# Pooled attention and a feed-forward in Strassen form: the first pass's sums, the Mish tiles and the written orders

## The chip, the cores and the metric

The program runs on one core of a Trainium2 chip. Counted is the device time in microseconds, median of three runs. The engines are TensorE (PE), VectorE (DVE), ScalarE (ACT), GpSimd (POOL) and SyncE (SP, which here only issues DMAs). Each works its own queue in order; semaphores tie the queues together.

## What is computed

```python
q_pool = q.reshape(B, H, S // 2, 2, D).mean(axis=3)          # B, H, S, D = 4, 8, 1152, 64
attn = softmax(q_pool @ k.T / sqrt(D))                       # per head, 576 x 1152
x = (attn @ v).transpose(0, 2, 1, 3).reshape(2304, 512)
h = x @ w_in                                                 # 512 -> 2048
out = (h * tanh(softplus(h))) @ w_out                        # Mish, 2048 -> 512
```

q, k, v and the output are float32, the two weights float64.

## The kernel before

**Attention.** 32 steps (four batches, four pairs of heads, two halves of the queries). A step i has nine chunks of keys. `QK(i, c)` forms scores in one of two PSUM tiles, `CP` (ACT) copies them to SBUF, `MX`/`MXF` (DVE) keep a running maximum, `MT`, `TMAX`, `MB` turn it into one maximum per query, `SUB` (DVE) and `EXP` (ACT) form the weights, `PV` (PE) multiplies by v, `ADD` (POOL, and for n = 2 a DMA that adds) sums the weights, `FIN0` (PE) adds them over the partitions, and `FLN`, `FEX`, `FC`, `FE`, `FT`, `FU`, `FX` divide and write the result into the large SBUF tile xT (512 x 2304, transposed). For the last two steps `LX` (DVE: an addition, a reciprocal, a product) does the division instead.

**Feed-forward, first pass (the border).** The tokens are cut in six tiles u of 256 for a start; with them the first two of sixteen column blocks f of w_in are done directly: `split_h`/`split_l` cut x into a high and a low part, `H_(u, f)` makes 12 matmuls of 128x256 into an h tile of PSUM (four buffers), `A_g` and `A_gh` (ACT) apply Mish twice (once in full into the SBUF tile g, once rounded into gh), `D_gl` (DVE) forms the rest gl = g - gh, and `O_(u, f)` makes 6 matmuls of 128x512 with w_out. `EVP(u, t)` (ACT) copies the partial sum of 128 tokens out of PSUM into a tile ev, and SP writes it to a DRAM tile part[n], n = 2u + t. The PSUM pairs of O_ take turns, so O_(u, 0) needs the copies of tile u - 2.

**Feed-forward, second phase.** Three groups tp of 768 tokens and eight pairs fp of column blocks make 22 units (tp, fp); the pairs fp = 0 of tp = 0 and 1 are the first pass. A unit is one 2x2 Strassen-Winograd product for the first layer. `XS(tp, n)` (DVE) forms the four differences T1 to T4 of x, each 128x768, from xT (T2 needs T1, T4 needs T2), in three buffers tf; `XH`/`XL` split them. `HP(u, i)` makes seven products of 6 matmuls of 128x384 in PSUM tiles ma, mb, mc; `CPY` and `CC` combine them; `GH` (rounded, to SBUF) and `GG` (in full, in place in PSUM) apply Mish and `GL` forms the rest. `OT(u, n)` makes 6 matmuls of 128x512 for each of six blocks of 128 tokens, with the columns of Gh and Gl as weights and woh, wol as the moving operand. `EV(u, n)` adds the block into xT, which now is the accumulator. Before the first unit of a group adds, `LDP(tp)` (SP) loads the group's six partial sums from part into xT. In group 0 the weights of each unit come as float64 halves in pieces of 512 KB (ri, ro; two buffers); `conv(n, m)` turns a piece into float32 (ACT for m = 0, 1, DVE for m = 2, 3), and conv(n, 3) also issues, on SP, the load of piece n + 2 and a write of the result to DRAM. `SS`, `WH`, `WL` form the unit's weights in the Strassen sums, high and low.

**Order.** The order is written out: each step has a due time in the lists FILL, STEP, END (attention), EDGE (the border, the first and last units of the groups) and STEADY (the units between, with a fixed distance of 15.42), the lists are sorted together, and each engine gets its steps in that order. Pools of SBUF grow from the left and from the right; `reuse_lead` closes the first pass's pools (x3, x2, ag, w0) and opens g, sixteen tiles of 1,536 bytes for Gh and Gl, directly below the pool xp.

The lines that the rows name: 163 QK, 173 CP, 184 MX, 188 MXF, 237 ADD, 267 FIN0, 294 the reciprocal in LX, 389 and 392 the loads of ro and ri, 429 to 454 conv, 992 H_, 996 A_g, 1000 A_gh, 1004 D_gl, 1022 O_, 1027 and 1028 EVP, 1057 XS, 1078 LDP, 1120 HP, 1134 GG, 1138 GH, 1141 GL, 1156 OT, 1165 and 1167 EV.

Of the kernel before, what the change touches and what calls it, by code (L numbers as in the profile page):

```python
# [8 lines left out]
F32 = mybir.dt.float32  # L9
# [9 lines left out]
def f32(ap):  # L19
    return ap.bitcast(F32)  # L20
# [3 lines left out]
def tile_pooled_attention_then_winograd_ffn(ctx: ExitStack, tc: tile.TileContext, q, k, v, moe_w_in, moe_w_out, out):  # L24
# [47 lines left out]
    if True:  # L72
# [1230 lines left out]
        EDGE = [  # L1303
            (-13.0330, FIN0, 28),
            (-12.6895, EXP, 30, 0),
            (-12.3201, PV, 29, 7),
            (-12.0293, FU, 27),
            (-11.8317, FT, 27),
            (-11.1537, EXP, 30, 1),
            (-10.9073, PVE, 29),  # L1310
            (-10.7457, MX, 31, 3),
            (-10.6938, MX, 31, 4),
            (-10.6866, QK, 31, 5),
            (-10.6568, FLN, 28),
            (-10.3955, SUB, 30, 2),
            (-10.0428, QK, 31, 6),
            (-9.8865, CP, 31, 5),
            (-9.8744, FX, 27),
            (-9.0670, ADD, 30, 0),
            (-8.9770, PV, 30, 0),  # L1320
            (-8.8741, FC, 28),
            (-8.5939, MX, 31, 5),
            (-8.4872, MX, 31, 6),
            (-8.4709, CP, 31, 6),
            (-8.3566, QK, 31, 8),
            (-8.2718, ADD, 29, 3),
            (-8.2711, FEX, 28),
            (-8.2122, QK, 31, 7),
            (-8.0969, SUB, 30, 3),
            (-7.8370, EXP, 30, 2),  # L1330
            (-7.8368, ADD, 29, 4),
            (-7.6090, CP, 31, 8),
            (-7.3915, MX, 31, 8),
            (-7.2454, MX, 31, 7),
            (-7.2076, reuse_qk),
            (-7.0445, PV, 30, 4),
            (-6.5484, PV, 30, 2),
            (-6.4867, split_h, 3, 2),
            (-6.0919, split_l, 3, 2),
            (-5.7490, PV, 30, 5),  # L1340
            (-5.7338, split_h, 3, 0),
            (-5.4196, CP, 31, 7),
            (-5.2127, PV, 30, 1),
            (-5.1721, ADD, 30, 1),
            (-5.1571, MXF, 31),
            (-4.6980, FE, 28),
            (-4.6428, split_h, 4, 0),
            (-4.5310, split_h, 3, 3),
            (-4.4512, FU, 28),
            (-3.9977, MT, 31),  # L1350
            (-3.5935, EXP, 30, 3),
            (-3.5625, ADD, 30, 2),
            (-3.3583, split_h, 4, 1),
            (-3.1474, FIN0, 29),
            (-3.1319, TMAX, 31),
            (-2.9496, split_h, 4, 2),
            (-2.5840, FLN, 29),
            (-2.4205, PV, 30, 3),
            (-2.4066, FEX, 29),
            (-2.1443, split_h, 3, 1),  # L1360
            (-1.9834, MB, 31),
            (-1.8885, SUB, 31, 0),
            (-1.8191, split_h, 4, 3),
            (-1.6307, PV, 30, 6),
            (-1.5130, EXP, 31, 0),
            (-1.2737, SUB, 31, 1),
            (-1.0879, SUB, 31, 2),
            (-0.4317, PV, 30, 7),
            (-0.0860, PV, 30, 8),
            (0.4023, PVE, 30),  # L1370
            (0.5731, EXP, 31, 1),
            (1.0951, H_, 1, 0),
            (1.2725, H_, 0, 1),
            (1.2827, PV, 31, 2),
            (1.9519, split_l, 3, 0),
            (2.1706, split_l, 4, 1),
            (2.2210, H_, 0, 0),
            (2.2881, split_l, 3, 1),
            (2.7888, SUB, 31, 3),
            (2.9710, split_l, 4, 3),  # L1380
# [60 lines left out]
            (16.8182, split_h, 5, 2),
            (16.8931, conv, 5, 1),
            (17.1764, conv, 4, 2),
            (17.2002, split_h, 5, 0),
            (17.3767, conv, 4, 3),
            (17.4440, split_h, 5, 3),
            (17.9332, conv, 5, 2),
            (17.9528, A_gh, 2, 0),
            (18.0820, split_l, 5, 1),
            (18.5279, conv, 5, 3),  # L1450
            (18.5785, O_, 1, 1),
            (18.6459, EVP, 1, 0),
            (18.8540, D_gl, 2, 0),
            (19.2055, H_, 3, 0),
            (19.4107, split_l, 5, 3),
            (19.8397, split_l, 5, 0),
            (20.3631, A_gh, 3, 1),
            (20.7401, split_l, 4, 2),
            (20.7904, A_g, 3, 0),
            (20.8692, H_, 4, 0),  # L1460
            (21.1001, O_, 2, 0),
            (21.5031, split_l, 5, 2),
            (22.0276, XS, 0, "T1"),
            (23.2741, D_gl, 2, 1),
            (23.6050, A_gh, 3, 0),
            (23.7571, XS, 0, "T2"),
            (23.7621, EVP, 0, 0),
            (23.8913, H_, 5, 1),
            (24.2332, XH, 0, "T1"),
            (24.2446, conv, 6, 0),  # L1470
            (24.6680, A_g, 4, 0),
# [660 lines left out]
```

## Time and profile before

| | us |
|---|---|
| median of 3 runs | 815.37 |
| lowest and highest | 813.34, 815.38 |
| the profiled execution | 812.05 |
| its span, first to last instruction | 810.3 |
| PE busy | 785.6 |
| DVE busy | 627.0 |
| ACT busy | 605.7 |
| POOL busy | 598.6 |

The rows further down come from the profiled execution. Attention ends near 422 us, the border runs to about 444, the units follow to 805. "Idle before" is the time for which the engine stood before an instruction, and behind the arrow stands what released it. PEclk is the granted share of TensorE's full clock (2.4 GHz). Matmuls overlap, so the time of one is read from the distance of two starts.

### The profile page before, as it was taken

To read this page: it belongs to the slowest core of one execution; us is meant where nothing else is said; L and a number is where in the kernel's file an instruction comes from. 1 tells how busy PE (TensorE), PEld (TensorE's weight loads), DVE (VectorE), ACT (ScalarE), POOL (GpSimd) and SP (SyncE) were. 2 spreads that over 40 slices of the span, in tenths; PEclk is the share of its full clock that TensorE was granted. 3 is DMA by queue.
4 is the path that set the end of the run, shared out by engine and by line. 5 is a ranking of instruction groups with operands and counts; after the bars stand their busy time and mean duration, and the time that the engine had idled before them with its cause. 6 is when DMAs were issued, how large, how long until landed. Compare 5 with 4: busy or idle time off the path is not lost.

```text
span 810.3 us, 13588 instructions
## 1 busy us (share of the span) xinstructions
PE 785.6 (97%) x4991; PEld 547.9 (68%) x4991; DVE 627.0 (77%) x809; ACT 605.7 (75%) x1026; POOL 598.6 (74%) x461
## 2 busy tenths in 40 slices
PE   7899999999999999999899799999999999999997
PEld 4455455555555554554478698898899888888985
DVE  5999999999999999999778579876564574245444
ACT  6999999999999999999857777776544564644441
POOL 4779998898898898898892756668765697666550
PEclk9999999999999999999999999999999999999999
DMA  7567557546656556555246866652722113311302
GB/s 261 161 164 192 134 133 176 121 135 151 156 144 170 118 139 147 137 141 105 59 88 215 294 206 195 213 165 79 194 78 80 53 52 129 106 53 52 104 27 78
DMA packets 47441, 109.40 MB, mean 135 GB/s; under 512 B 3984, under 2 KB 19600, under 8 KB 47376
## 3 DMA queue, kind: packets, MB, share of 16 engines
q1 hardware_dynamic: 37584, 58.99, 22.5%
q0 software_dynamic: 4608, 28.31, 17.8%
q10 hardware_dynamic: 5184, 21.24, 7.8%
q8 instruction: 39, 0.64, 0.3%
q14 instruction: 26, 0.21, 0.1%
HBM read 63.96 MB, written 16.25 MB: 99 GB/s over the span
## 4 chain that ended last, share of the span: by engine, by line
PE 82%; DMA 5%; DVE 5%; POOL 3%; ACT 2%; issue 2%; SPq 0%; ACTq 0%; DVEq 0%; POOLq 0%
PE O L1156 22%; PE s L163 19%; PE pv L245 16%; PE ma L1120 11%; PE mc L1120 6%; PE mb L1120 3%; PE Sb L267 2%; DMA acc<-TB 2%; PE mt L199 2%; DMA ri<-in_moe_w_in_dram 1%; DVE rmax L184 1%; DMA part<-ev 1%; PE Mb L216 1%; POOL acc L237 1%; DVE TA L222 1%
## 5 line engine op out<-in xcount | busy, mean ns | idle before, releaser
L163 PE MATMUL s<-qT,kT 64*128 64x288 f32 x1152 | 204.2, 451 | 4.8 <-ACT TA L173 2.5
L163 PEld LDWEIGHTS s<-qT,kT 64*128 64x128 f32 x1152 | 92.5, 187 | 101.3 <-DVE rmax L184 27.2
L173 ACT COPY TA<-s 128x576 f32<-128x576 f32 x192 | 117.8, 638 | 22.4 <-PE s L163 16.0
L222 DVE TENSOR_TENSOR TA<-TA,Mb 128x1152 f32<-128x1152 f32 x96 | 128.9, 1347 | 1.7 <-PE Mb L216 0.8
L1167 DVE TENSOR_TENSOR xT<-xT,O 128x512 f32<-128x512 f32 x126 | 83.4, 683 | 50.3 <-PE O L1156 49.1
L245 PE MATMUL pv<-TA,vn 128*64 128x288 f32 x768 | 115.7, 422 | 1.4 <-ACT TA L226 1.3
L226 ACT ACTIVATE TA<-TA 128x1152 f32<-128x1152 f32 x96 | 112.8, 1176 | 2.4 <-DVE TA L222 1.8
L231 POOL TENSOR_TENSOR acc<-TA 128x1152 f32<-128x1152 f32 x32 | 85.0, 2657 | 35.5 <-PE s L163 19.0
L1156 PE MATMUL O<-woh,Gh 128*128 128x512 f32 x264 | 104.5, 396 | 2.4 <-DVE xT L1167 2.3
L1156 PE MATMUL O<-woh,Gl 128*128 128x512 f32 x264 | 104.4, 395 | 0.0
L1156 PE MATMUL O<-wol,Gh 128*128 128x512 f32 x264 | 104.3, 395 | 0.0
L1088 POOL TENSOR_TENSOR wS<-wS 128x256 f32<-128x256 f32 x84 | 64.9, 780 | 46.6 <-DMA wS<-spill 38.7
L184 DVE TENSOR_TENSOR rmax<-s,rmax 128x576 f32<-128x576 f32 x128 | 93.2, 749 | 2.1 <-ACT TB L173 0.9
L237 POOL TENSOR_TENSOR acc<-acc 128x576 f32<-128x576 f32 x64 | 91.8, 1434 | 3.9 <-DMA acc<-TB 2.6
L1101 POOL TENSOR_TENSOR wol<-wO,woh 128x1024 fp32r<-128x1024 f32 x22 | 54.3, 2468 | 38.1 <-ACT woh L1097 38.1
L245 PEld LDWEIGHTS pv<-TA,vn 128*64 128x64 f32 x768 | 47.1, 137 | 49.0 <-issue 9.1
L1101 POOL TENSOR_TENSOR wbl<-wS,wbh 128x1024 fp32r<-128x1024 f32 x22 | 53.0, 2407 | 28.3 <-ACT wbh L1097 28.3
L1124 ACT COPY s<-ma 128x384 f32<-128x384 f32 x44 | 21.1, 481 | 66.3 <-PE ma L1120 66.3
L222 DVE TENSOR_TENSOR TB<-TB,Mb 128x1728 f32<-128x1728 f32 x32 | 62.2, 1944 | 0.0
L173 ACT COPY TB<-s 128x576 f32<-128x576 f32 x96 | 59.7, 654 | 2.3 <-DVE rmax L184 2.1
L245 PE MATMUL pv<-TB,vn 128*64 128x288 f32 x384 | 61.1, 414 | 0.0
L1156 PEld LDWEIGHTS O<-woh,Gh 128*128 128x128 f32 x264 | 49.5, 187 | 13.3 <-DVE xT L1167 3.7
(236 smaller groups left out, 1766.9 us busy)
## 6 DMA issues: line engine op xcount, KB each, us to landing
acc<-TB POOLq DMA_DIRECT2D x32, 864.0 KB, 6.3
ri<-in_moe_w_in_dram SPq DMA_DIRECT2D x16, 512.0 KB, 4.0
ro<-in_moe_w_out_dram SPq DMA_DIRECT2D x16, 512.0 KB, 4.1
wS<-spill SPq DMA_DIRECT2D x30, 256.0 KB, 2.9
wO<-spill SPq DMA_DIRECT2D x30, 256.0 KB, 4.1
qn<-in_q_dram ACTq DMA_DIRECT2D x12, 576.0 KB, 5.6
kT<-in_k_dram ACTq DMA_DIRECT2D x12, 576.0 KB, 3.9
vn<-in_v_dram ACTq DMA_DIRECT2D x12, 576.0 KB, 4.2
```

The lines of the kernel that those rows point to most:

```text
L163: pe.matmul(s[:, j, 0:HQ], kT[64 * j:64 * j + 64, c], qT[64 * j:64 * j + 64, hf], start=True, stop=True,)
L173: act.copy(T(i, c), ss[i, c])
L184: dve.tensor_tensor(ss[i, c] if c == FOLD else r, ss[i, c], x, ALU.max)
L222: dve.tensor_tensor(x, x, Mbs[i].unsqueeze(1).to_broadcast([P, w, W]), ALU.subtract)
L226: act.activation(x, x, AF.Exp, scale=0.0625)
L231: pool.tensor_tensor(accs[i][:, 0:2], T(i, 0, 2), T(i, 2, 4), ALU.add)
L237: pool.tensor_tensor(accs[i][:, 0], accs[i][:, 0], accs[i][:, n - 2], ALU.add)
L245: pe.matmul(pvs[i][64 * j:64 * j + 64, 0:HQ], vn[:, j, c, :], T(i, c)[:, j], start=(pvn[i] == 1), stop=(pvn[i] == NC),)
L1101: (dve if e == "dve" else pool).tensor_tensor(l, w_part(u, q), f32(h), ALU.subtract)
L1120: pe.matmul(o, a, b, start=(new and m == 0), stop=(last and m == len(seq) - 1), skip_group_check=True)
L1156: pe.matmul(o, x, y[:, f], start=(f == 0 and m == 0), stop=(f == 1 and m == 2))
L1167: dve.tensor_tensor(acc, acc, o, ALU.add)
```

## The change

`EVP` for n < 6, the tokens of group 0, copies its partial sum straight into xT; nothing is written to part and `LDP(0)` is gone (`LDP(1)` stays). All four T differences have a buffer of their own. The copies overwrite what XS reads, so XS T1, T2, T4 now stand before the first EVP and T3 before the others. `A_g` works in place in the h tile, after `A_gh`, and `D_gl` reads g from PSUM; the SBUF tiles g (four of 1,024 bytes) are gone. A pool pad of 64 bytes is opened between xp and g, so that all Gh and Gl tiles lie 64 bytes lower. EDGE and both lists of STEADY get new times, which changes the order on all engines from step 31 of the attention on; the steps are the same but for LDP(0).

```diff
-        def A_g(u, f):
-            ch[u, f] = pools["ag"].tile([P, UT], F32, tag="g", name=f"g{u}_{f}")
-            act.activation(ch[u, f], hs[u, f], AF.Mish)
-
         def A_gh(u, f):
             gs[u, f] = [pools["ag"].tile([P, UT], F32R, tag="gh", name=f"gh{u}_{f}")]
             act.activation(gs[u, f][0], hs[u, f], AF.Mish)
 
+        def A_g(u, f):
+            act.activation(hs[u, f], hs[u, f], AF.Mish)
+
         def D_gl(u, f):
             gl = pools["ag"].tile([P, UT], F32R, tag="gl", name=f"gl{u}_{f}")
-            dve.tensor_tensor(gl, ch.pop((u, f)), f32(gs[u, f][0]), ALU.subtract)
+            dve.tensor_tensor(gl, hs[u, f], f32(gs[u, f][0]), ALU.subtract)
             gs[u, f].append(gl)
...
         def EVP(u, t):
             n = u * (UT // P) + t
+            if n < KT:
+                act.copy(xT[:, :, n * P:(n + 1) * P], os_[u][t].rearrange("p (a b) -> p a b", b=P))
+                return
             e = pools["ev"].tile([P, DM], F32, tag="ev", name=f"ev{n}")
...
-            t = pools["xt"].tile([P, 2, TH], F32, tag="tf", bufs=3, name=f"{n}f{tp}")
+            t = pools["xt"].tile([P, 2, TH], F32, tag="tf", bufs=4, name=f"{n}f{tp}")
...
         def reuse_lead():
             close("x3", "x2", "ag", "w0")
+            open_pool("pad", 1, side="right").tile([P, 16], F32, name="pad")
             open_pool("g", 8, side="right")
...
-            (42.2186, LDP, 0),
...
```

Of the orders, what the prediction speaks of, by engine. PE from step 31's last chunk on: before H_(1,0), H_(0,1), ..., FIN0(31), O_(0,0), O_(0,1), O_(1,0), O_(1,1), ...; after H_(0,1), H_(1,1), ..., H_(0,0), H_(1,0), ..., O_(0,0), ..., O_(0,1), H_(2,0), FIN0(31), O_(1,0), O_(1,1), H_(2,1), H_(3,0), H_(3,1), H_(4,0), O_(2,0), O_(2,1). DVE after LX(31): before conv(4,1), ..., XS T1, T2, T3 later and T4 after the last gl but one; after XS T1, conv(4,1), XS T2, XS T4, conv(4,2), ..., XS T3. ACT in the border: after, EVP(1,0), EVP(0,1), EVP(0,0) stand behind split_h(5,3) and ahead of A_g(3,0) and A_gh(3,1). ACT in steps 30 and 31: after, the copies CP(31, 5) and (31, 6) stand ahead of EXP(30, 2) and of FC(28) and FLN(28).

## Rows read from the trace of the kernel before

**Rows 1.** The page, part 1: busy time of the engines.

```profile
PE 785.6 (97%) x4991; PEld 547.9 (68%) x4991; DVE 627.0 (77%) x809; ACT 605.7 (75%) x1026; POOL 598.6 (74%) x461
```

**Rows 2.** Table of stretches: busy time by engine, PEclk, DMA share, GB/s.

```profile
393.00:400.00 7.00, 4.81 (x24) 1.94 (x24) 5.63 (x7) 5.69 (x11) 6.58 (x5) 0.82 0.01 2
...
444.00:461.00 17.00, 15.17 (x75) 13.11 (x74) 9.48 (x14) 12.80 (x26) 15.11 (x10) 1.00 0.90 278
461.00:466.00 5.00, 1.22 (x7) 0.88 (x5) 2.37 (x5) 3.13 (x6) 0.90 (x1) 0.98 0.97 370
466.00:471.00 5.00, 4.88 (x20) 4.88 (x21) 3.11 (x6) 2.35 (x5) 3.87 (x2) 0.68 0.78 244
...
650.00:800.00 150.00, 148.43 (x726) 130.88 (x725) 73.97 (x122) 73.72 (x139) 90.66 (x62) 1.00 0.22 71
800.00:811.00 11.00, 4.75 (x19) 3.23 (x18) 2.75 (x4) 0.00 (x0) 0.00 (x0) 0.98 0.50 143
```

**Rows 3.** Waits of PE, 370 to 500 us: total, times, longest.

```profile
PE mb L1120 <- DVE Gl L1141: 3.9, 1, 3.9
```

**Rows 4.** The chain of waits, 408 to 480 us: start, duration, what.

```profile
412.68 6.88 DMA acc<-TB
...
428.96 1.45 PE h L992 x12
...
466.12 2.29 PE mb L1120 x6
...
469.88 1.04 PE mc L1120 x6
```

**Rows 5.** Timeline of DVE, 424 to 482 us: start, duration, operation, idle before.

```profile
451.71 0.69 DVE L436 SCALAR_TENSOR_TENSOR wS<-cw,wS 128x512 int32<-128x512 int32 x1 [0.59 <-ACT cw L429]
...
463.52 0.69 DVE L434 SCALAR_TENSOR_TENSOR wO<-ro,cl 128x512 int32<-128x512 int32 x1 [5.29 <-ACT cl L432]
```

**Rows 6.** Timeline of ACT, the same stretch.

```profile
462.87 0.62 ACT L432 ACTIVATE cl<-ro 128x512 int32<-128x512 uint16 x1 [4.15 <-DMA ro<-in_moe_w_out_dram]
```

**Rows 7.** Timeline of SP, the same stretch.

```profile
451.62 4.45 SPq L1078 DMA_DIRECT2D xT<-part  x6
456.18 0.66 SPq L389 DMA_DIRECT2D ro<-in_moe_w_out_dram  x1
```

**Rows 8.** Groups of instructions, whole run: count, busy us, mean ns, idle before.

```profile
L1156 PE MATMUL O<-woh,Gh 128*128 128x512 f32 x264 | 104.5, 396 | 2.4 <-DVE xT L1167 2.3
...
L1141 DVE TENSOR_TENSOR Gl<-mb,Gh 128x384 fp32r<-128x384 f32 x44 | 24.3, 552 | 31.5 <-ACT mb L1134 31.5
...
L1134 ACT ACTIVATE mb<-mb 128x384 f32<-128x384 f32 x44 | 21.4, 487 | 0.0
...
L1004 DVE TENSOR_TENSOR gl<-g,gh 128x256 fp32r<-128x256 f32 x12 | 10.1, 871 | 4.7 <-ACT gh L1000 4.2 <-ACT g L996 0.5
...
L294 DVE RECIPROCAL rs<-rs 128x288 f32<-128x288 f32 x2 | 3.9, 1952 | 0.1
...
L1165 ACT COPY xT<-O 128x512 f32<-128x512 f32 x6 | 3.5, 590 | 3.0 <-PE O L1156 3.0
```

**Rows 9.** Timeline of PE, 438 to 448 us: O_ in the border.

```profile
441.61 0.39 PE L1022 MATMUL o<-wh,gh 128*128 128x512 f32 x1
...
444.11 0.39 PE L1022 MATMUL o5pv<-wh,gl 128*128 128x512 f32 x1
...
445.38 0.40 PE L1022 MATMUL o5x<-wh,gh 128*128 128x512 f32 x1
...
446.54 0.40 PE L1022 MATMUL o5pv<-wh,gl 128*128 128x512 f32 x1
```

**Rows 10.** Line 1057, whole run: count, then least, median and longest in ns.

```profile
L1057 DVE TENSOR_TENSOR T1f<-xT x3: 947/2258/2902, 431.2 to 589.5; 128x768 f32<-128x768 f32 x3
```

**Rows 11.** Timeline of PE, 500 to 533 us: twelve O in a row.

```profile
508.31 0.39 PE L1156 MATMUL O<-woh,Gh 128*128 128x512 f32 x1
...
510.88 0.40 PE L1156 MATMUL O<-woh,Gl 128*128 128x512 f32 x1
```

More of the change, by code (lines that the diff above doesn't have):

```diff
@@ L1342, in tile_pooled_attention_then_winograd_ffn @@
[L1342 to L1356, printed above, removed]
@@ L1460, in tile_pooled_attention_then_winograd_ffn @@
[L1460 to L1471, printed above, removed]
-            (25.2107, XS, 0, "T3"),
-            (25.3005, D_gl, 3, 1),
@@ new lines, in tile_pooled_attention_then_winograd_ffn @@
+            (-5.4141, split_h, 3, 0),
+            (-5.3593, PV, 30, 2),
+            (-5.0877, PV, 30, 5),
+            (-4.7548, MT, 31),
+            (-4.3208, split_h, 3, 3),
+            (-3.9867, FIN0, 29),
+            (-3.7802, TMAX, 31),
+            (-3.7620, PV, 30, 1),
+            (-3.7457, MB, 31),
+            (-3.6748, H_, 0, 1),
+            (-3.5729, EXP, 30, 3),
+            (-3.3188, split_h, 4, 2),
+            (-3.1558, SUB, 31, 0),
+            (-2.9851, SUB, 31, 1),
+            (-1.6340, split_h, 4, 1),
@@ new lines, in tile_pooled_attention_then_winograd_ffn @@
+            (9.1237, FT, 29),
+            (9.1719, PV, 31, 0),
+            (9.6329, A_g, 1, 1),
+            (9.6389, D_gl, 1, 1),
+            (9.6892, FX, 28),
+            (10.3157, O_, 0, 0),
+            (10.4126, A_g, 0, 1),
+            (10.7814, FU, 29),
+            (11.0789, ADD, 31, 3),
+            (11.4486, A_g, 1, 0),
+            (12.2864, D_gl, 0, 1),
+            (12.3515, PV, 31, 5),
+            (12.3709, ADD, 31, 4),
+            (12.6535, PV, 31, 7),
+            (12.7131, FIN0, 30),
@@ new lines, in tile_pooled_attention_then_winograd_ffn @@
+            (12.7593, O_, 0, 1),
+            (13.0887, split_h, 3, 1),
+            (13.4056, H_, 2, 0),
+            (13.5472, D_gl, 1, 0),
+            (13.7810, split_l, 3, 1),
+            (14.0541, split_l, 3, 2),
+            (14.1979, PVE, 31),
+            (14.7597, A_gh, 2, 0),
+            (15.1099, LX, 30),
+            (15.3407, FIN0, 31),
+            (15.6302, A_g, 2, 0),
+            (15.9459, D_gl, 2, 0),
+            (15.9681, FX, 29),
+            (15.9723, LX, 31),
+            (16.9759, reuse_rest),
@@ new lines, in tile_pooled_attention_then_winograd_ffn @@
+            (20.0316, H_, 3, 0),
+            (20.2955, conv, 4, 2),
+            (20.4654, H_, 3, 1),
+            (20.4860, A_gh, 3, 0),
+            (20.5399, split_h, 5, 3),
+            (20.8124, conv, 5, 1),
+            (20.9698, conv, 4, 3),
+            (21.2842, EVP, 1, 0),
+            (21.3403, EVP, 0, 1),
+            (21.5302, conv, 5, 2),
+            (21.7328, H_, 4, 0),
+            (22.1500, conv, 5, 3),
+            (22.6481, EVP, 0, 0),
+            (22.6558, A_g, 3, 0),
+            (22.9148, D_gl, 2, 1),
@@ new lines, in tile_pooled_attention_then_winograd_ffn @@
+            (27.4788, A_g, 4, 0),
+            (28.2972, split_l, 5, 3),
+            (28.3443, EVP, 1, 1),
+            (28.5573, H_, 4, 1),
+            (28.6896, conv, 6, 0),
+            (28.8027, A_gh, 4, 1),
+            (29.0491, split_l, 5, 2),
+            (29.3600, EVP, 2, 1),
+            (29.4304, D_gl, 3, 1),
+            (29.5355, O_, 3, 0),
+            (29.7139, O_, 3, 1),
+            (29.9214, XH, 0, "T1"),
+            (30.1471, SS, (0, 1), "S2", "dve"),
+            (30.2051, split_l, 5, 0),
@@ new lines, in tile_pooled_attention_then_winograd_ffn @@
+            (30.2194, EVP, 3, 0),
+            (30.5239, conv, 7, 0),
+            (30.7660, A_g, 4, 1),
+            (31.1285, SS, (0, 1), "S4", "dve"),
+            (31.5615, conv, 6, 1),
+            (32.0989, H_, 5, 0),
+            (32.1581, conv, 6, 2),
+            (32.3502, XH, 0, "T4"),
+            (32.8328, H_, 5, 1),
+            (33.0606, conv, 6, 3),
+            (33.3144, conv, 7, 1),
+            (33.5147, EVP, 2, 0),
+            (33.6361, A_gh, 5, 0),
+            (33.6996, conv, 7, 2),
@@ new lines, in tile_pooled_attention_then_winograd_ffn @@
+            (33.7588, EVP, 3, 1),
+            (33.8930, D_gl, 4, 1),
+            (34.0693, A_g, 5, 0),
+            (34.1945, XL, 0, "T4"),
+            (34.4557, WH, (0, 1), "a"),
+            (34.4794, A_gh, 5, 1),
+            (34.7735, D_gl, 4, 0),
+            (34.8552, conv, 7, 3),
+            (35.0139, A_g, 5, 1),
+            (35.1494, O_, 4, 0),
+            (35.8183, O_, 4, 1),
+            (36.1439, XH, 0, "T3"),
+            (36.2459, XL, 0, "T1"),
+            (36.2636, D_gl, 5, 1),
@@ new lines, in tile_pooled_attention_then_winograd_ffn @@
+            (36.3440, D_gl, 5, 0),
+            (36.8079, reuse_psH),
+            (37.2951, WL, (0, 1), "a", "dve"),
+            (37.3145, O_, 5, 0),
+            (37.3822, WH, (0, 1), "b"),
+            (37.7796, EVP, 4, 0),
+            (37.7871, WH, (0, 1), "o"),
+            (37.9767, O_, 5, 1),
+            (38.3152, conv, 8, 1),
+            (38.3359, EVP, 5, 0),
+            (38.8071, conv, 8, 0),
+            (40.3194, conv, 8, 2),
+            (40.7814, conv, 8, 3),
+            (41.0742, WL, (0, 1), "b"),
@@ new lines, in tile_pooled_attention_then_winograd_ffn @@
+            (44.6527, reuse_lead),
+            (44.8606, EVP, 4, 1),
+            (44.9545, EVP, 5, 1),
+            (44.9817, CPY, (0, 1), 1),
+            (45.3261, SS, (0, 2), "S1"),
+            (45.4095, CC, (0, 1), 1),
+            (45.6380, HP, (0, 1), 4),
+            (46.2528, GH, (0, 1), 0),
+            (46.3762, SS, (0, 2), "S2"),
+            (46.4546, GG, (0, 1), 0),
+            (46.9984, WH, (0, 2), "a"),
+            (47.0440, WL, (0, 1), "o"),
+            (47.3187, GL, (0, 1), 0),
@@ new lines, in tile_pooled_attention_then_winograd_ffn @@
+            (151.8994, GH, (1, 1), 0),
+            (152.1183, XL, 1, "T3", "pool"),
+            (154.2877, GG, (1, 1), 0),
+            (154.3742, XL, 1, "B22", "dve"),
+            (154.5425, HP, (1, 1), 5),
+            (154.9658, HP, (1, 1), 4),
+            (155.0034, GL, (1, 1), 0),
+            (156.3818, EV, (0, 7), 4),
+            (156.7558, LDP, 1),
+            (156.8362, OT, (0, 7), 5),
+            (156.9700, XH, 1, "T4"),
+            (158.8649, CC, (1, 1), 1),
+            (159.2732, CC, (1, 1), 3),
@@ new lines, in tile_pooled_attention_then_winograd_ffn @@
+            (159.3097, GH, (1, 1), 1),
+            (159.3332, EV, (0, 7), 3),
+            (159.4496, GG, (1, 1), 1),
+            (159.5087, GH, (1, 1), 3),
+            (159.5095, XL, 1, "T4", "pool"),
+            (159.6982, GG, (1, 1), 3),
+            (159.7103, HP, (1, 1), 6),
+            (160.9491, GH, (1, 1), 2),
+            (161.3276, GL, (1, 1), 3),
+            (161.6041, GL, (1, 1), 1),
+            (161.6515, OT, (1, 1), 0),
+            (163.3596, EV, (0, 7), 5),
+            (163.6658, GG, (1, 1), 2),
```

1312 lines of the change are left out of this document (593 added, 719 removed).

## The prediction

> **What bounds the kernel now.** I read the page's first part, then the table of stretches, then TensorE's waits. TensorE (PE) is busy 785.6 us of a span of 810.3 [rows 1]; no other engine comes near. Even from 650 to 800 us, deep in the units, it stands still for 1.57 of 150 us only [rows 2]. A change that leaves the matmuls as they are can gain in two ways only: by the 25 us in which PE idles or runs slow, or by a shorter time from one matmul to the next.
>
> The idle time sits in few places [rows 2]. From 393 to 400 us, the last attention steps, PE idles 2.19 us at a mean granted clock of 0.82. From 444 to 461 it idles 1.83. From 461 to 466 it idles 3.78, and 466 to 471 runs at 0.68. After 800 it idles 6.25, most of it the last output's way out. The longest single wait, 3.9 us, is the matmul group mb behind Gl on VectorE (DVE) [rows 3]. When it ends, six mb matmuls take 2.29 us where six mc just after take 1.04 [rows 4]: the clock had fallen to its lower level (1.2 of 2.4 GHz) after the idle stretch.
>
> What made Gl late: DVE stood 5.29 us before a conversion, waiting for ScalarE (ACT) [rows 5]; ACT stood 4.15 us for the weight piece ro [rows 6]; and SyncE (SP) could issue ro only at 456.18, behind six loads xT<-part that took its queue from 451.62 for 4.45 us [rows 7]. These six are LDP(0), which brings the first pass's partial sums back from DRAM. The conversion that allows ro's load had begun at 451.71 and takes 0.69 [rows 5]. So ro was issued about 3.8 us after it could have been: 456.18 - 452.40.
>
> **Part by part, against the profiled execution (812.05 us, of which 810.3 is span; the median of the three runs is 815.37, 3.3 above it).**
>
> *Partial sums straight into xT.* Removed: six writes to part, six reads back (12 x 256 KB, 3 MB in a stretch whose DMA engines are 90 to 97% busy [rows 2]) and the 4.45 us on SP. With ro issued 3.8 us earlier, Gl ends 3.8 us earlier, and the wait of 3.9 shrinks to about 0.1. The slow clock behind it goes too: six mb cost 2.29 - 1.04 = 1.25 more and the mean 0.68 of [rows 2] gives 5 x 0.32 = 1.6 lost in all. Gain 3.8 + 1.6 = **5.4 us**; lower bound 0 (if another wait stands there, below), upper bound 7.2 (if the 1.83 of 444 to 461 goes as well). I take 5.4: the 1.83 comes from other chains, copies and sums of the first unit, which the change keeps. The copies themselves are as long as before: a copy of this shape from PSUM into xT takes 0.59 [rows 8], and the one it replaces writes the same 128x512.
>
> Added: the copy may only overwrite xT when T1 to T4 have been formed from it. So XS T1, T2 and T4 move ahead on DVE, behind LX(31), and ACT, which works its queue in order, has the copies EVP(1,0), (0,1), (0,0) at its head until T4 is there, with the Mish of later tiles queued behind. PE needs the first pair of PSUM tiles back for O_(2,0). Cover: behind FIN0(31) PE has two O_ of six matmuls (12 x 0.227 = 2.73 by the starts of [rows 9]) and four H_ of 1.45 [rows 4], 8.5 us. Against it: LX(31), a reciprocal of 1.95 [rows 8] and two short operations that I take at Gl's 0.55; three XS at 0.95 (the least in [rows 10]); one short conversion at 0.55; three copies at 0.59. Sum 1.95 + 1.1 + 2.85 + 0.55 + 1.77 = 8.2. It fits by 0.3 us. At the longest XS there, 2.90, three cost 5.9 more. So the cost is 0 to 5.6; I take 0, since in this border XS ran at 0.95, POOL being idle for most of it.
>
> *Mish in place.* The same number of ACT operations, PSUM to PSUM; the form stands in the second phase: 128x384 in 0.487 [rows 8]. gl is then formed from PSUM, as Gl is, 0.552 for 384 columns [rows 8], against 0.871 for 256 columns when both operands lie in SBUF. Twelve of them: 12 x 0.3 = 3.8 us of DVE time saved or, at the other end, nothing. DVE is not what PE waits for there, so the sum takes 0. The price is that an h buffer stays occupied until gl is formed; four buffers, and the new order asks for the fifth (H_(2,0)) only after O_(0,1), when its gl must be done anyway: 0. The Trainium skill (SBUF — State Buffer, Who interferes with whom) says that a VectorE operation with two SBUF inputs contends with a GpSimd one that reads SBUF, and that one with a single SBUF input does not; the 0.871 against 0.552 agrees. By that rule the 3.8 us of DVE would be sure; the sum would not change.
>
> *Reordering of the border.* Before MT(31), ACT's copies of scores 5 to 8 move ahead of the statistics of step 28, so their PSUM returns sooner; the sums of step 31 and their DMA move up on POOL. FIN0(31) is the last attention matmul; it waited for POOL behind a transfer of 6.88 [rows 4]. Bounds: nothing, or all of the 393 to 400 loss, 2.19 + 7 x 0.18 = 3.4. I take **1.5**, near the middle, because the 6.88 us transfer stays in the chain and only its start moves.
>
> *Orders in the steady units.* PE hardly waits there, so the most that a better order can give is the 1.57 of 650 to 800 [rows 2]; a worse one could add as much again. The matmuls are the same. I take 0.
>
> *The 64 bytes.* G lies directly under the pool xp, 8 x 2 tiles of 1,536 bytes; the pad moves all of it down by 64. Consecutive O matmuls start (510.88 - 508.31) / 11 = 0.2336 us apart [rows 11]. O_ of the border, the same 128x512 form, runs at (444.11 - 441.61) / 11 = 0.2273 in a long run and at (446.54 - 445.38) / 5 = 0.232 in a run of six [rows 9]. At 2.4 GHz 6.3 ns are 15 columns, or 60 bytes of a float32 row. By the sizes of the pools the weights (gh) and the moving operand (wh) of O_ start a multiple of 512 bytes apart, while Gh (167,904) and woh (80,544) are 87,360 = 341 x 256 + 64 apart; the pad makes it 341 x 256. I read this as: the spacing depends on the two addresses, and the pad brings O to O_'s. 792 matmuls (three groups of 264, one of them in [rows 8]): at most 792 x 6.3 = 5.0 us, at least 792 x 1.6 = 1.3 if it works as in short runs. Most runs of O are six or twelve long, so I take 3.4 ns: **2.7 us**.
>
> Sum: 5.4 + 1.5 + 2.7 = 9.6 us. On the median, 815.4 - 9.6 = **805.8 us** (802.4 on the profiled execution).
>
> **The rivals.** *The spacing is no matter of address.* For it: short runs of O_ at 0.232 are almost O's. Against: the long run's 0.2273 is steady over eleven steps, and O's 0.2336 too. Then 815.4 - 6.9 = 808.5. The Trainium skill stands on this side: SBUF — State Buffer says that PE never waits on anyone and gives 16-byte lines, of which 64 bytes are a whole number; by that the pad is worth nothing. The 0.2336 against 0.2273 of one form speaks against the rule.
>
> *The wait comes back elsewhere in the first unit.* With Gl early, the next late thing may be the lower halves from POOL (XL, WL) or the first unit's sums, which made the 1.83. If half of the 5.4 is lost again: 808.5 with the pad's gain, 811 without.
>
> *Slower: the copies into xT block ACT.* If POOL works while XS runs, each XS may take 2.90 [rows 10]. Four of them are 7.8 us late, 7.5 past the cover; PE idles at O_(2,0) and again at O_(3,0) or O_(4,0), and each such stop costs about 1.6 more by the lower clock. Cost 7.5 + 3.2 = 10.7 against 6.9 gained: 819 with no gain from the pad. It turns the sign once XS takes over 2 us on average. Against it: three XS in a row took 0.95 in this border.
>
> **How the numbers follow.** Forecast (stall gone, spacing shorter) 0.55, own range 801 to 809; spacing unchanged 0.22, 808.5; stall back in part 0.12, 808 to 811; all of it swallowed, near no change, 0.06, 814 to 816; slower 0.05, 819. The range 800.5 to 811 leaves out the last two and what lies under 800.5, which takes the full 5.0 of the pad with 7.2 and 3.4 at once. About 0.3% (2.4 us) is what a measurement of this kernel tells from no change. Faster 0.89, same 0.06, slower 0.05.
>
> **What would show it.** No xT<-part load before the first unit, and no PE wait over 1 us for Gl near 460; full clock from the border's end on. XS T1, T2, T4 before the copies, each near 0.95, and PE not idle before O_(2,0). O starts 0.227 to 0.232 apart; if they stay at 0.2336 or rise, that step is wrong. It would be wrong as a whole if PE idles over 5 us between 393 and 480.

## The result, and the profile after

| | before | changed |
|---|---|---|
| median, us | 814.36 (4 runs, 812.47 to 815.38) | **803.62** (4 runs, 802.24 to 804.83) |
| ratio to before, 95% interval | | **0.987** (0.9843 to 0.9897) |
| the profiled execution, its span | 812.05, 810.3 | 804.83, 803.1 |

The change gained 10.7 us by the medians; 9.6 were forecast. First the page's busy times, as in [rows 1], and the table of stretches, as in [rows 2] (us; busy time of PE, PEld, DVE, ACT, POOL with counts; granted clock; DMA share; GB/s), both of the changed kernel:

```profile
PE 781.0 (97%) x4991; PEld 546.0 (68%) x4991; DVE 621.7 (77%) x809; ACT 605.7 (75%) x1026; POOL 594.4 (74%) x461
```

```profile
393.00:400.00 7.00, 4.52 (x28) 1.79 (x28) 5.04 (x7) 5.63 (x9) 3.68 (x3) 1.00 0.48 95
444.00:461.00 17.00, 16.13 (x80) 14.04 (x79) 11.91 (x19) 16.42 (x32) 16.18 (x12) 1.00 0.85 265
461.00:466.00 5.00, 5.00 (x27) 4.56 (x26) 3.14 (x6) 3.49 (x6) 2.73 (x2) 1.00 0.95 311
466.00:471.00 5.00, 5.00 (x29) 4.75 (x28) 3.67 (x7) 4.27 (x10) 4.18 (x5) 1.00 0.75 242
650.00:800.00 150.00, 147.19 (x722) 130.02 (x721) 72.14 (x121) 70.98 (x136) 86.94 (x61) 1.00 0.23 71
```

From 461 to 471 PE is busy throughout at full clock, where it had idled 3.78 us and then run at 0.68. From 393 to 400 it still idles, 2.48 us now. The clock there, 0.82 before and 1.00 here, is no gain of the order: in that stretch e1 and e4, both with the attention's order of before, ran at 1.00 and 0.73, and e2, with the new one, at 0.83. (The last stretch holds the end of the last unit, which comes earlier now, so its idle time is not that of [rows 2].)

The waits of PE from 370 to 500 us, as in [rows 3] (total, times, longest), name no Gl any more:

```profile
PE s L163 <- ACT TA L173: 1.9, 4, 0.8
PE mt L199 <- DVE rmax L188: 1.1, 1, 1.1
PE s L163 <- DVE rmax L184: 1.0, 1, 1.0
PE ma L1122 <- DVE mb L1130: 0.8, 1, 0.8
PE Sb L267 <- POOL acc L237: 0.2, 1, 0.2
```

SP's timeline, as in [rows 7], has both ro loads at once and no load of partial sums between them:

```profile
450.71 0.33 SPq L389 DMA_DIRECT2D ro<-in_moe_w_out_dram  x1
452.14 0.33 SPq L389 DMA_DIRECT2D ro<-in_moe_w_out_dram  x1
```

**Where the time went.** Three matmuls that both kernels have cut the span: the group mt near 387 us (attention, ahead of all reordered steps that matter), FIN0(31), and the first mb of the group that waited for Gl; as many matmuls start before it, 3341, in either trace. PE's timeline of the changed kernel:

```profile
388.76 0.76 PE L199 MATMUL mt<-identr,rmax 64*128 64x64 f32 x10
...
424.78 0.70 PE L267 MATMUL Sb<-acc,cst 128*64 128x288 f32 x4 [0.24 <-POOL acc L237]
...
463.09 0.34 PE L1122 MATMUL mb<-xhp,wah 128*128 128x384 f32 x1
```

The same of the kernel before, whose mb stands at 466.12 [rows 4]:

```profile
386.53 0.69 PE L199 MATMUL mt<-identr,rmax 64*128 64x64 f32 x8
...
422.58 0.70 PE L267 MATMUL Sb<-acc,cst 128*64 128x288 f32 x4 [0.47 <-POOL acc L237]
```

All kernels below are read in this way:

| us | start to mt | mt to FIN0(31) | FIN0(31) to mb | mb to the end |
|---|---|---|---|---|
| before | 386.5 | 36.05 | 43.54 | 344.1 |
| changed | 388.8 | 36.01 | 38.31 | 340.0 |
| e9, changed again | 387.7 | 36.02 | 38.32 | 339.5 |
| e1, pad alone | 387.2 | 35.83 | 44.51 | 342.2 |
| e10, weights moved | 386.3 | 36.43 | 44.07 | 341.3 |
| e2, pad of 128 | 387.5 | 36.89 | 38.36 | 339.9 |
| e3, pad of 192 | 387.2 | 36.01 | 38.41 | 341.2 |
| e4, loads later | 386.4 | 36.95 | 41.87 | 342.9 |
| e6, sums through DRAM | 386.9 | 36.02 | 48.32 | 344.4 |
| e5, copies first | 385.7 | 34.51 | 38.34 | 339.2 |
| e11, copies first, pad of 320 | 388.3 | 34.52 | 38.32 | 339.5 |
| e8, g in SBUF | 387.5 | 36.57 | 42.15 | 339.4 |
| e12, loads later, Mish in PSUM, old order | 386.5 | 40.03 | 45.27 | 344.4 |
| e7, old order at the first change of group | 385.8 | 36.01 | 38.29 | 358.7 |

The first column is the same program in all of them: it ends up to 0.9 us earlier or 2.2 later than in the profile of before, decided in the first 30 us. No edit touches that code, and the two profiles of the changed kernel differ by 1.1, so I take it for chance. The changed kernel's first profile drew the latest start of all, so its span is only 7.2 us shorter; without the first column it is 9.4. The border from FIN0(31) on gave 5.2, what follows 4.2, and the tail of the attention nothing.

The other columns have some chance in them too. The border of e1 and e10 is that of the kernel before, and takes 44.51 and 44.07: PE waits 1.3 and 0.9 us for a gl there, which it does not in the profile of before. So the border's gain lies between 5.2 and 6.2. The wait in e1:

```profile
PE o3x L1022 <- DVE gl L1004: 1.3, 1, 1.3
```

The tail takes 35.8 to 37.0 in the old order (without e12) and 36.0 to 36.9 in that of the change, and every value above 36.03 belongs to a trace with a lowered clock from 393 to 400.

### The profile page after: what moved, and what is told of

Read it like the earlier page. It is cut to its first block, busy times and chain, and to the rows that moved or that the text cites. A ratio compares the mean times of both kernels' runs of the same rounds, so it can differ in the third digit from the quotient of the medians.

```text
span 803.1 us, 13565 instructions
## 1 busy us (share of the span) xinstructions
PE 781.0 (97%) x4991; PEld 546.0 (68%) x4991; DVE 621.7 (77%) x809; ACT 605.7 (75%) x1026; POOL 594.4 (74%) x461
## 4 chain that ended last, share of the span: by engine, by line
PE 82%; DVE 5%; POOL 4%; DMA 4%; ACT 2%; issue 2%; SPq 0%; ACTq 0%; DVEq 0%; POOLq 0%
PE O L1158 22%; PE s L163 20%; PE pv L245 16%; PE ma L1122 11%; PE mc L1122 6%; PE mb L1122 3%; PE Sb L267 2%; DMA acc<-TB 2%; PE mt L199 2%; POOL acc L237 1%; DVE rmax L184 1%; PE Mb L216 1%; POOL acc L231 1%; DVE TA L222 1%; PE h L992 1%
## 5 line engine op out<-in xcount | busy, mean ns | idle before, releaser
L1143 DVE TENSOR_TENSOR Gl<-mb,Gh 128x384 fp32r<-128x384 f32 x44 | 24.4, 554 | 43.9 <-ACT mb L1136 43.8
```

## Experiments

Ratios are to the kernel before, run on the same chip beside each; e2, e3 and e10 are single executions, read for their traces.

| | median, us | ratio, 95% interval |
|---|---|---|
| e1 | 811.74 | 0.9967 (0.9948 to 0.9987) |
| e4 | 811.1 | 0.9956 (0.9939 to 0.9973) |
| e5 | **800.14** | **0.9835** (0.9812 to 0.9858) |
| e6 | 816.44 | 1.002 (0.9999 to 1.0041) |
| e7 | 819.78 | 1.008 (1.005 to 1.0109) |
| e8 | 807.08 | 0.9905 (0.988 to 0.993) |
| e9 | 803.27 | 0.987 (0.9848 to 0.9893) |
| e11 | 802.12 | 0.985 (0.983 to 0.987) |
| e12 | 816.27 | 1.0018 (1.0005 to 1.0032) |
| e2, e3, e10 | 804.5, 804.54, 809.94 | |

### The 64 bytes: e1, e2, e3, e10

e1 gives the kernel before the pad and nothing else:

```diff
             close("x3", "x2", "ag", "w0")
+            open_pool("pad", 1, side="right").tile([P, 16], F32, name="pad")
             open_pool("g", 8, side="right")
```

> The kernel before with the 64-byte pad under pool g and nothing else. Theory (the start-to-start time of O depends on the addresses of weights and moving operand): the mean of O's spacings under 245 ns falls from 233.1 to 229.7 ns as in the changed kernel, and the time by about 2.6 us, ratio 0.997; the stall of 3.9 us for Gl stays. Rival (the shorter spacing comes from the new order or from less traffic): spacing stays at 233.1, ratio 1.000.

e2 and e3 change the pad's size in the changed kernel (`[P, 32]` and `[P, 48]`):

> The changed kernel with a pad of 128 bytes instead of 64, so Gh and woh start 341 x 256 - 64 bytes apart. If what counts is the distance of the two addresses modulo 128, O's spacing is back at 233.1 ns and the time near 806 us. If any shift of the pool away from its old place is enough, the spacing stays at 229.7 and the time near 803.6.

> The changed kernel with a pad of 192 bytes: the distance of Gh and woh is 0 modulo 128 and 128 modulo 256. If the period is 128 bytes, O's spacing stays at 229.7 ns. If the period is 256 or more, it lies at or near 233.1 ns and the time near 806 us.

e10 moves the other operand instead, in the kernel before, and with it the pools that are opened behind wf (the T differences, ev and the copies of CPY):

```diff
             close("p3", "p2", "p1")
+            open_pool("pad", 1).tile([P, 16], F32, name="pad")
             open_pool("wf", 1)
```

> The kernel before with a 64-byte pad under pool wf instead of pool g: woh and wol move up by 64 bytes, Gh and Gl stay where they were. Their distance is then 256 modulo 512, as in the changed kernel, while Gh's own address is that of before. If the distance of the two operands counts, O's spacing falls from 233.1 to about 229.7 ns. If the place of Gh alone counts, it stays at 233.1; if that of woh alone counts, any value may come.

Measured: the mean distance from a start of O to the start of the next matmul, over those some 780 of the 792 in each trace that are under 245 ns. The second column is the distance of Gh and woh in SBUF by the tiles' places. The last two are the means within runs of 6 and of 24 O that no other matmul interrupts.

| | (Gh - woh) mod 256 | mean, ns | runs of 6 | runs of 24 |
|---|---|---|---|---|
| before | 64 | 233.1 | 233.0 | 233.3 |
| changed (64) | 0 | 229.7 | 230.5 | 229.1 |
| e1 (64, nothing else) | 0 | 229.6 | 230.4 | 228.4 |
| e10 (woh up by 64) | 0 | 230.0 | 230.7 | 228.4 |
| e11 (320; 0 mod 512 too) | 0 | 229.6 | 230.5 | 229.0 |
| e2 (128) | 192 | 230.2 | 231.5 | 229.6 |
| e3 (192) | 128 | 232.7 | 232.9 | 232.8 |

Twelve O in a row, first and last, as in [rows 11], first in the changed kernel:

```profile
504.77 0.39 PE L1158 MATMUL O<-woh,Gh 128*128 128x512 f32 x1
...
507.31 0.39 PE L1158 MATMUL O<-woh,Gl 128*128 128x512 f32 x1
```

The same in e10:

```profile
508.74 0.39 PE L1156 MATMUL O<-woh,Gh 128*128 128x512 f32 x1
...
511.27 0.39 PE L1156 MATMUL O<-woh,Gl 128*128 128x512 f32 x1
```

And in e3:

```profile
503.44 0.39 PE L1158 MATMUL O<-woh,Gh 128*128 128x512 f32 x1
...
505.99 0.39 PE L1158 MATMUL O<-woh,Gl 128*128 128x512 f32 x1
```

That is 2.54 / 11 = 0.2309, 2.53 / 11 = 0.2300 and 2.55 / 11 = 0.2318 us, against 0.2336 of before. The rows are rounded to 0.01 us, which is 0.9 ns in such a quotient, so the means of the table are what counts. Traces with the same places agree: 233.1 in before, e4 and e12, 229.7 or 229.8 in the changed kernel and in e5 to e9.

What follows: the spacing is a matter of the places of tiles in SBUF, shown by e1 with no other change. The distance of the two operands would explain e10 too, which shortens the spacing with Gh where it was; but e10 moved more than woh and wol. Read by distance, the period is neither 128 (e3 would be short) nor 512 (e11 would be shorter than the change). But "a multiple of 256" isn't the rule either: e2, 64 bytes off on the other side, is nearly as short. Of its two expectations "any shift is enough" comes nearest, and e3 rules that out. Nor is the distance of a matmul's own operands all: in e10 the products with T2l and T4l went from 177.6 and 179.0 to 174.1 and 175.6 ns, though T and their weights moved together; and in e1, where only Gh and Gl moved, those with T4l went from 179.0 to 175.8 and those of T4h with the weights' high part from 175.2 to 178.2. The mechanism stays open. In time, e1 gives 0.0033 x 814.15 = 2.7 us (1.1 to 4.2 by its interval), and the sum of all 792 distances falls from 188.1 to 185.5 us.

### The loads of the partial sums: e4, e6

e4 leaves everything in the kernel before but the due time of six loads, which now comes behind that of conv(9, 3):

```diff
-            (42.2186, LDP, 0),
+            (42.6621, LDP, 0),
             (42.3729, conv, 9, 0),
...
             (42.6620, conv, 9, 3),
```

> The kernel before with one thing moved: the six loads of the partial sums are issued behind the load of the weight piece ro instead of ahead of it; the same bytes are moved. Theory (place on SyncE's queue): ro is issued near 452.4 instead of 456.2 us, the wait of mb for Gl shrinks from 3.9 to under 1 us and the six mb run at 1.05 to 1.3 instead of 2.29 us; ratio 0.993 to 0.995. Rival (the 3 MB of traffic, which only leaving the transfers out removes): ro lands late all the same, at least half of the 3.9 us stays, ratio 0.997 or above.

Measured: 0.9956, 3.6 us by the ratio. SP's timeline of e4:

```profile
453.24 0.33 SPq L389 DMA_DIRECT2D ro<-in_moe_w_out_dram  x1
454.79 4.73 SPq L1078 DMA_DIRECT2D xT<-part  x6
```

DVE's, at the first EV:

```profile
464.00 0.69 DVE L1167 TENSOR_TENSOR xT<-xT,O 128x512 f32<-128x512 f32 x1 [1.69 <-DMA xT<-part]
464.61 0.55 DVE L1141 TENSOR_TENSOR Gl<-ma,Gh 128x384 fp32r<-128x384 f32 x1
```

And PE's:

```profile
465.21 0.45 PE L1120 MATMUL mb<-xhp,wah 128*128 128x384 f32 x1 [1.45 <-DVE Gl L1141]
```

The place on SP's queue was indeed the larger part: ro goes first, the wait is 1.45 instead of 3.91 us, and the six mb run at the full rate (the stretch to the end is 1.3 us shorter, as much as they had lost). What is left is the other cause: the sums themselves land late, DVE stands 1.69 us for them at the first EV, and Gl stands behind that on DVE. Neither expectation held whole; the changed kernel, which leaves the transfers out, has neither wait. The granted clock is of note: it fell to 0.68 behind a stop of 3.9 us [rows 2, 3], and stays at 1.00 behind one of 1.45, as the table of stretches of e4 has it:

```profile
461.00:466.00 5.00, 3.55 (x18) 2.93 (x17) 3.21 (x6) 2.31 (x5) 3.60 (x2) 1.00 1.11 357
466.00:471.00 5.00, 5.00 (x30) 4.84 (x29) 3.09 (x6) 4.67 (x9) 2.40 (x1) 1.00 0.93 313
```

The length of the stop alone does not decide it: in e12 the clock fell behind a stop of 1.94 us (mean 0.66 over the next 5 us), in e6 it stayed at 1.00 behind one of 2.0.

e6 puts the sums through DRAM again in the changed kernel:

```diff
-            if n < KT:
-                act.copy(xT[:, :, n * P:(n + 1) * P], os_[u][t].rearrange("p (a b) -> p a b", b=P))
-                return
...
+            (43.1640, LDP, 0),
             (43.1650, conv, 9, 3),
```

> The changed kernel with the six first partial sums again written to DRAM and loaded back, the loads ahead of the weight piece's load on SyncE as before; orders, Mish in PSUM and pad as changed. Theory (the stall went because the loads left SyncE's queue): ro is issued 3 to 4.5 us later and a PE wait of 2 to 4 us with a slow stretch comes back between 455 and 470: near 808 us, ratio 0.990 to 0.994. Rival (the new order of the first unit alone hid the stall): 803.6, ratio 0.987.

Measured: 12 to 13 us slower than the changed kernel, more than either theory said. ACT's timeline of e6 in the border:

```profile
436.95 0.59 ACT L1026 COPY ev<-o 128x512 f32<-128x512 f32 x1 [5.88 <-DMA part<-ev]
```

PE's, at the same time:

```profile
437.59 0.80 PE L1021 MATMUL o<-wh,gh 128*128 128x512 f32 x1 [5.33 <-ACT ev L1026]
```

SP's, 20 us later:

```profile
457.86 4.65 SPq L1077 DMA_DIRECT2D xT<-part  x6
462.62 0.58 SPq L389 DMA_DIRECT2D ro<-in_moe_w_out_dram  x1
```

And ACT's, when that ro has landed:

```profile
469.32 0.62 ACT L432 ACTIVATE cl<-ro 128x512 int32<-128x512 uint16 x1 [4.34 <-DMA ro<-in_moe_w_out_dram]
```

The stall for ro came back as the first theory said (ACT 4.34 us, PE 2.0 for Gl). The larger loss is new: the order puts three EVP in a row behind T4, there are two buffers ev, and the third copy waits 5.88 us for a write to DRAM; PE stands 5.33 us for the PSUM tile. So the order of the change leans on copies that need no buffer and no transfer. FIN0(31) to mb: 48.3 us, against 43.5 with old order and DRAM, 38.3 with new order and none.

### The tail of the attention: e5

In the changed order DVE's MX(31, 3) stands ahead of ACT's CP(31, 3), and MX(31, 4) ahead of CP(31, 4): both only read the scores in one PSUM tile, and the later in program order waits for the earlier. e5 turns the two pairs round:

```diff
-            (-13.0793, MX, 31, 3),
+            (-13.0500, MX, 31, 3),
...
-            (-12.5726, MX, 31, 4),
+            (-12.5400, MX, 31, 4),
```

> The changed kernel with MX(31,3) and MX(31,4) put back behind CP(31,3) and CP(31,4) in program order, nothing else. Theory (the border's reorder gained nothing because ACT's copy waits in its PSUM bank for DVE's maximum, 2.11 us): that wait is gone, EXP(30,0) begins about 2 us earlier, and 1 to 2 us of the border come back: near 802 us, ratio to the kernel before 0.984 to 0.986. Rival (the transfer acc<-TB of 6.88 us sets FIN0(31) however the copies stand): the wait goes but the time stays at 803.6, ratio 0.987.

Measured: 0.9835, the fastest of all. ACT's timeline at CP(31, 3) in the changed kernel:

```profile
394.37 0.64 ACT L173 COPY TA<-s 128x576 f32<-128x576 f32 x1 [2.11 <-DVE rmax L184]
394.91 1.17 ACT L226 ACTIVATE TA<-TA 128x1152 f32<-128x1152 f32 x1
```

The same in e5:

```profile
389.46 0.64 ACT L173 COPY TA<-s 128x576 f32<-128x576 f32 x1 [0.31 <-PE s L163]
390.00 1.17 ACT L226 ACTIVATE TA<-TA 128x1152 f32<-128x1152 f32 x1
```

Counted from each kernel's mt (388.76 and 385.65), the copy begins at 5.61 and 3.81 us: 1.8 earlier, and EXP behind it too. PE's rows of e5:

```profile
385.65 0.76 PE L199 MATMUL mt<-identr,rmax 64*128 64x64 f32 x10
...
420.16 0.70 PE L267 MATMUL Sb<-acc,cst 128*64 128x288 f32 x4 [0.40 <-POOL acc L237]
```

mt to FIN0(31) is 34.51 us instead of 36.01, and 34.52 in e11, which has the same order. The transfer of 6.88 us stays in the chain (6.86 in e5, 6.88 in e11). The rival fell: it is not the transfer's length but its start that sets FIN0(31). By the trace e5 is worth 1.5 us; its median is 3.5 lower than the changed kernel's, its early start being part of that, and side by side e11 is 1.2 lower than e9. The intervals of the ratios overlap with those of the change, so the gain rests on the two traces.

### Mish in place: e8, e12

e8 gives the changed kernel the SBUF tile g again (two buffers, for want of room):

```diff
-            act.activation(hs[u, f], hs[u, f], AF.Mish)
+            ch[u, f] = pools["ag"].tile([P, UT], F32, tag="g", bufs=2, name=f"g{u}_{f}")
+            act.activation(ch[u, f], hs[u, f], AF.Mish)
...
-            dve.tensor_tensor(gl, hs[u, f], f32(gs[u, f][0]), ALU.subtract)
+            dve.tensor_tensor(gl, ch.pop((u, f)), f32(gs[u, f][0]), ALU.subtract)
```

> The changed kernel with Mish's result g again in an SBUF tile of its own (two buffers), so gl is formed from two SBUF operands; all else as changed. Theory (DVE is not what TensorE waits for in the border): gl takes 0.8 to 0.9 us instead of 0.42, twelve of them about 5 us of DVE, and the time stays within 1 us of the changed kernel, ratio 0.986 to 0.988. Rival (those 5 us of DVE now matter, because the new order leaves T1, T2 and T4 between the gl): waits of O_ for gl of 2 to 5 us in all, 806 to 809 us, ratio 0.990 to 0.994.

Measured: 807.08 us beside 803.27 of e9, 3.8 slower; FIN0(31) to mb 42.15 instead of 38.3. My theory of no cost fell. The group gl of the changed kernel (count | busy, mean ns | idle before):

```profile
L1003 DVE TENSOR_TENSOR gl<-h,gh 128x256 fp32r<-128x256 f32 x12 | 4.7, 418 | 5.4 <-ACT h L999 5.4
```

DVE's timeline of e8, gl from SBUF:

```profile
437.35 0.42 DVE L1004 TENSOR_TENSOR gl<-g,gh 128x256 fp32r<-128x256 f32 x1
...
442.03 4.04 DVE L1004 TENSOR_TENSOR gl<-g,gh 128x256 fp32r<-128x256 f32 x2
```

POOL's, at the same time as the last row:

```profile
442.00 1.84 POOL L1072 TENSOR_TENSOR T4l<-T4f,T4h 128x768 fp32r<-128x768 f32 x1 [14.03 <-ACT T4h L1068]
443.80 1.98 POOL L1072 TENSOR_TENSOR T1l<-T1f,T1h 128x768 fp32r<-128x768 f32 x1
```

And a wait of PE in e8:

```profile
PE o L1022 <- DVE gl L1004: 2.4, 1, 2.4
```

With two SBUF operands gl takes 0.42 us where POOL rests (five of the twelve in e8) and 0.74 to 2.35 where it meets POOL at work. The mean of 0.871 in [rows 8] hid these two kinds: seven of 0.42, one of them beside POOL, and five of 1.01 to 2.18. From PSUM all twelve take 0.42, beside POOL too. This is the contention of which the Trainium skill speaks (SBUF — State Buffer, Who interferes with whom): a VectorE operation with two SBUF inputs contends with a GpSimd one that reads SBUF. The trace agrees, and here it lies on the path. Some of the 3.8 us is the experiment's own: with two buffers ACT waits 3.7 us in all for g's buffers.

e12 takes the kernel before with e4's loads and Mish in PSUM, without the other edits (A_g behind A_gh; H_(2, 0) and H_(2, 1) had to go behind the gl whose PSUM buffer they take):

```diff
...
-            (7.3085, H_, 2, 0),
-            (7.6131, H_, 2, 1),
+            (8.3358, H_, 2, 0),
+            (11.2319, H_, 2, 1),
...
```

> The kernel before with the loads of the partial sums behind ro's load (as in e4) and Mish in place in PSUM, without the pad, the copies into xT and the new orders; A_g stands right behind A_gh, and H_(2,0) and H_(2,1) behind the gl whose PSUM buffer they take. Theory (the gl from two SBUF operands, 2.2 us where POOL works beside them against 0.42, hold up the first unit): no gl over 0.6 us, the wait of o3x for gl (0.9 us in e4) and most of the 1.4 us for Gl go; ratio 0.990 to 0.993. Rival (in-place Mish is worth something only under the new order): ratio as in e4, 0.9945 to 0.997, or above it where H_ now comes later.

Measured: 1.0018, so Mish in PSUM, with the order of H_ that it forces, costs 5 us here (816.27 against 811.1 of e4; 8 by the two traces), and my theory fell again. All gl take 0.42 to 0.43 us, as expected, but of PE's waits over the whole run one line has grown (1.1 us in e4) and one is new:

```profile
PE Sb L267 <- POOL acc L237: 3.1, 2, 2.5
...
PE h L992 <- DVE gl L1003: 2.8, 1, 2.8
```

An h buffer is now occupied until gl is formed. H_ waits 2.8 us for one, and the two H_ that stood ahead of FIN0(30) no longer fill PE's time there: it waits 2.5 for POOL's sum. The clock is lower as well: 0.90 from 444 to 461 and, as said, 0.66 behind the wait for Gl, which is 1.94 us here. Taken together: in the new order Mish in PSUM is worth up to 3.8 us; in the old one, with H_ moved back, it costs 5.

### The order at the first change of group: e7

The first trace of the changed kernel lost 1.0 us between 544 and 556 us, with a wait of mc for ACT of 0.64. e7 sets 131 entries of EDGE (units (0, 7) and (1, 1), and XS, XH, XL, LDP of group 1) back to their old times.

> The changed kernel with the order of before in the change from token pass 0 to 1 (131 entries of the order list, from the last unit of pass 0 and the first of pass 1). Theory (the new order there costs the 1.0 us that appears at 545 to 556 us, at a wait of mc for ACT's copy): the trace gains 1 us there, near 802.6 us, ratio 0.986. Rival (the 1.0 us is a shift that later work gives back, or comes from the units in front): no change, ratio 0.987, or slower where old and new orders meet.

Measured: 16 us slower, all behind mb (358.7 us instead of 340). PE's waits of e7:

```profile
PE O L1158 <- DVE xT L1169: 7.5, 4, 5.0
```

Old and new times don't mix, I take it: the old entries come into the new ones of the units around them. O stands 5.0 us for an addition on DVE. The run says nothing on the 1.0 us. Part of that is chance: in e9, the same kernel, the loss is 0.6, and in e5 0.3.

### The change again, and a faster version: e9, e11

> The changed kernel once more, beside the two others: 803.6 us, ratio 0.987. In its first profile the work was 2.2 us late from 30 us on, in code that is the same in both kernels; if that is chance, it is not late again, and its span falls by 1 to 3 us while the median of the runs stays.

> The version of the copies ahead of the maxima with a pad of 320 bytes instead of 64: the distance of Gh and woh is then 0 modulo 512 as for the border's O_, instead of 256. If the period is 512, O's spacing falls from 229.7 to 228.6 ns, 0.9 us in all: 799.5 us, ratio 0.982. If it is 256, spacing and time are those of 64 bytes: 229.7 ns, 800.1 to 802 us, ratio 0.9835 to 0.985.

e9: 803.27 us and a span of 801.5, the start 1.1 us later than before's instead of 2.2; the other three columns repeat within 0.5 us. e11: 802.12, ratio 0.985, spacing 229.6: the larger pad is worth nothing, so e5 stands as the best version, with a pad of 64 bytes and the two copies ahead of their maxima. Its 0.9835 and e11's 0.985 are two measurements of what is in effect one kernel.

## Why the prediction was right, and where it was not

- **Total.** Forecast 805.8, range 800.5 to 811; measured 803.62, faster. By the three matmuls the change gained 9.4 (the profile of before is 2.3 us faster than that kernel's median, so this is a low value): the border with the slow clock behind it 6.5 instead of 5.4, the spacing 2.6 instead of 2.7, the rest of the units 0.3 instead of 0, the tail of the attention 0 instead of 1.5. So that the sum is near is partly luck: two errors, in the border and in the tail, went against each other.
- **Partial sums into xT (5.4).** Nearly right as a size: FIN0(31) to mb is 5.2 us shorter, the wait of 3.91 is gone, and so is the slow clock behind it (six mb had lost 1.25); 6.5 in all, within 0 to 7.2. The step "With ro issued 3.8 us earlier, Gl ends 3.8 us earlier, and the wait of 3.9 shrinks to about 0.1" is too simple. e4 does just that and keeps 1.45, because DVE also waited for the sums themselves, which the wait for ro had hidden. Three edits share the gain: the queue, the transfer (e4, e6) and Mish in PSUM (e8); no run has the copies into xT alone, so what they are worth by themselves stays open.
- **XS ahead of the copies (0).** Right. DVE's timeline of the changed kernel:

```profile
428.72 0.95 DVE L1059 TENSOR_TENSOR T1f<-xT 128x768 f32<-128x768 f32 x1
429.92 0.95 DVE L1059 TENSOR_TENSOR T2f<-xT,T1f 128x768 f32<-128x768 f32 x1
430.90 0.96 DVE L1059 TENSOR_TENSOR T4f<-xT,T2f 128x768 f32<-128x768 f32 x1
```

  ACT's, right behind it:

```profile
431.91 0.59 ACT L1026 COPY xT<-o1x 128x512 f32<-128x512 f32 x1
432.39 1.08 ACT L1026 COPY xT<-o 128x512 f32<-128x512 f32 x2
```

  The three run at their least [rows 10], the copies follow at once, and PE has no wait before O_(2, 0). The slower rival needed XS over 2 us.
- **Mish in place (0).** Wrong. "DVE is not what PE waits for there" holds in the profile of before, but in e1, e4 and e10, whose border has the old order too, PE waits 0.9 to 1.3 us for a gl, and in the new order e8 shows up to 3.8 us. I had the rule and the rows (0.871 against 0.552) and took only their mean; five gl of 1.01 to 2.18 us stood in the trace. The price, an h buffer occupied longer, was rightly put at 0 for the new order, where no H_ waits; e12 pays it in the old one.
- **Border (1.5).** Wrong as to the change, which gained nothing from mt to FIN0(31) (36.05 and 36.01); right as to what was there to be had, for e5 gains 1.5. The failed step is "ACT's copies of scores 5 to 8 move ahead of the statistics of step 28, so their PSUM returns sooner": I looked at what moved on ACT's queue and not at which of two readers of one tile comes first in program order. The upper bound also counted the lower clock from 393 to 400 as a loss to be had, and that comes and goes with the execution.
- **Steady orders (0).** Right on the whole. From mb to the end 4.2 to 4.6 us are gained; 1.25 are the slow mb, 2.6 the spacing, which leaves 0.3 to 0.8. By equal matmuls of both traces 0.3 to 1.0 us are lost at the first change of group and about 1.1 gained at the second, which nearly cancels.
- **The pad (2.7).** Right in size, measured 2.7 in e1 and 2.6 by the gaps. The middle value of 3.4 ns was met exactly (233.1 to 229.7). The reason was half right: the places count (e1); a multiple of 256 is not the rule (e2), and why they count stays open.

The rival that the spacing is no matter of address fell with e1. The rival that the stall comes back in part is the nearest to what a smaller change would have met: e4 has it, with a wait for the sums in place of the wait for ro.

## What to carry to other kernels

A stall often has a second one behind it that its own length hides: ask what would be late next, on the engine whose queue holds the late work, before crediting one cause with the whole. When readers of one PSUM tile on two engines are reordered, look at their order among each other; turning two pairs round was worth as much here as the whole planned reordering of the border. Edits that share buffers and an order (here copies, Mish in PSUM and the new times) have no price each: undone singly, DRAM sums cost 12 and Mish in SBUF 4 us, and Mish in PSUM done without the rest, with H_ moved back, costs 5.

## What the runs showed of the hardware

- The distance of starts of one matmul form (128x512, float32) depends on where tiles lie in SBUF: 229.6 to 230.2 ns or 232.7 to 233.1, by pads of 64 to 320 bytes below either operand. No wait appears in any trace for it. Products of 128x384 whose own operands stayed in place shifted by some 3 ns too (e1).
- ACT's read of a PSUM tile stood 2.11 us for DVE's read of the same tile that came first in program order. That two readers of one bank are kept apart is a rule of the Trainium skill (PSUM — Partial Sum Buffer, PSUM bank collisions raise a hardware error); the trace agrees and gives it a price.
- Code that is the same in all kernels ended between 0.9 us earlier and 2.2 us later by 30 us into the run. Stretches between named matmuls repeat far better: FIN0(31) to mb within 0.12 us over six kernels with the new border (38.29 to 38.41). But not everywhere: with the old border three kernels that are equal there took 43.54 to 44.51, and the tail of the attention varies by up to 0.9 us with the clock granted from 393 to 400.
